# Raw first weights loaded by an account of bytes, and their narrowed halves split by ScalarE and GpSimd, in a talking-heads attention with two feed-forward layers

## The chip, the cores and the metric

The kernel runs on one core of a Trainium2 chip. The metric is device time in microseconds (us). Engines are named as in the profile: PE is the matrix engine (PEld its weight loads), DVE is VectorE, ACT is ScalarE, POOL is GpSimd, SP issues most of the DMAs; SPq and POOLq are the queues of DMA issues on SP and GpSimd.

## What is computed

```python
scores = einsum('bhij,hg->bgij', scale * q @ k.T, w_pre)      # batch 4, 12 heads, 448 positions, 64 wide
attn = exp(scores - max); attn = attn / (sum(attn) + 1e-9)
x = einsum('bhij,hg->bgij', attn, w_post) @ v                 # as 1792 tokens x 768
h = x @ w_in                                                  # w_in 768 x 1024
solu = h * softmax(h)
x = ((solu - mean) / sqrt(var + 1e-6) * g_ln) @ w_out         # w_out 1024 x 768
out = relu(x @ w2_in)**2 @ w2_out                             # 768 x 2048 and 2048 x 768
```

The four weight matrices of the two layers reach the kernel as 64-bit numbers. The program narrows them to 32 bits by shifts and masks. The layers' products are taken with each operand as a high part and a low part (`hi`, `lo`).

## The kernel before

**Work units.** The attention is cut into 16 chunks of 120 or 88 query rows. A chunk's scores of all heads are laid out in `ssrc`; DMAs then gather them, 9 or 10 query rows x 12 heads at a time, into 180 blocks (`sdst`, `shuffle`, L214). Two blocks make a pair, and a loop (L563) runs over slots; slot `s` is the turn that finishes pair `s`, for s = 0 to 89.

**One slot** issues, in this order: loads of keys, queries and values that are due; the gathers of pair s+5 (SP queue, 2 x 210 KB); a store of a finished chunk (`x_out`); at most one raw load of the first layer's weights (`load_w1`, POOL queue, 256 KB); the first mix over heads for pair s+2 (`pre`, PE, L237); the copies of pair s-1's result out of PSUM (`post_out`, DVE, L321 and L326); products of queries and keys for a later chunk (`qk`, PE L203, ACT L210); maximum (DVE L248) and exponential (ACT L255) of pair s+2; in about every third slot half a chunk's product with the values (`av`, PE L341); the weights of the second mix for pair s+1 (`weigh`); the steps of the narrowing; and the second mix of pair s (`post`, PE L302, 64 matmuls). Since every pair has just 64 matmuls of L302, the first of them dates the slot in the trace. The engines take their instructions in order, and each may run ahead of the others as far as the data allow.

**Narrowing the first layer's weights.** There are 48 pieces of 128x256. A piece is loaded (`load_w1`, at most six ahead of the narrowing), squared by ACT two slots later (`start_w1`, L76), shifted and masked by three DVE steps that `filler()` hands out (L79, L83, L87; five calls in a slot with `av`, two in the first six slots), finished by two POOL operations (`flush`, L96, L97), scaled by ACT where it belongs to `w_out` (L410), and stored to memory (`store_w1`, SP queue, 128 KB). Raw, square and result live in rings of 7, 4 and 7 buffers.

**Splitting the narrowed weights.** `prep_first` (L421) reads `w_in` back in 24 pieces of 256 columns and two token tiles of x in three pieces each. For a piece it issues the load (SP), and five steps later a cast to `hi` (ACT and DVE in turn, L450) and a subtraction to `lo` (POOL, L451). Six steps run after the last narrowed piece is stored, the rest four to a slot from slot 80 on, when the memory of keys and queries is free. The first product of the layer (`h1`, L463) starts in slot 88.

**`weigh`** (L262) takes the reciprocal of the row sums and scales `w_post` by it: three POOL operations (L266, L267, L273), but for the last seven pairs two DVE operations and two of ACT:

```python
        if s < tail:                                     # tail = NP - 7
            nc.gpsimd.tensor_scalar(...)                 # L266
            nc.gpsimd.tensor_tensor(..., op=ALU.pow)     # L267
        else:
            nc.vector.tensor_scalar(...)                 # L269
            nc.vector.reciprocal(sm, sm)                 # L270
```

After slot 90 the two layers follow (L640 on), which the change does not touch.

Of the kernel before, what the change touches and what calls it, by code (L numbers as in the profile page):

```python
# [18 lines left out]
def kernel(  # L19
# [129 lines left out]
    tail = NP - 7  # L149
# [112 lines left out]
    def weigh(s):  # L262

        sm = sms.pop(s)
        if s < tail:
# [6 lines left out]
        if s < tail:
            nc.gpsimd.tensor_tensor(  # L273
                out=w.rearrange("p b g i -> p b (g i)"),
                in0=wpost_bd.rearrange("p g i -> p (g i)").unsqueeze(1).to_broadcast([128, 2, H * RH]),
                in1=sm.unsqueeze(2).to_broadcast([128, 2, H * RH]),
                op=ALU.mult,
            )
# [115 lines left out]
    def narrow_w1(i):  # L394
# [24 lines left out]
    QW = 256  # L419

    def prep_first():  # L421

# [4 lines left out]
        for i in range(len(todo) + ahead):
            if i < len(todo):
                cc, u = todo[i]
                r = wi1_p.tile([128, QW], F32, tag="wraw", name="wraw", bufs=6)  # L430
                if cc is not None:
                    if u == 0:
                        w1i.append((wi1b_p if cc else wi1_p).tile([128, 2, F1], F32R, name=f"w1i{cc}"))
                    t = w1i[cc]
                    src = w1iD[cc * 128:(cc + 1) * 128, u * QW:(u + 1) * QW]
                    dst = [t[:, a, u * QW:(u + 1) * QW] for a in range(2)]
                    nc.sync.dma_start(out=r, in_=src)
                    rv = r
                else:
                    x, u = divmod(u, 3)  # L440
                    if u == 0:
                        xs[x] = (wi1b_p if x else wi1_p).tile([128, 2, CC, 128], F32R, name=f"xs{x}")
                    src = xD[u * 256:(u + 1) * 256, x * 128:(x + 1) * 128].rearrange("(c p) t -> p c t", p=128)
                    dst = [xs[x][:, a, 2 * u:2 * u + 2] for a in range(2)]
                    rv = r.rearrange("p (c t) -> p c t", c=2)
                    nc.sync.dma_start(out=rv, in_=src)
# [116 lines left out]
    for s in range(lo_s, NP + 2):  # L563
# [471 lines left out]
```

## Time and profile before

| | |
|---|---|
| three runs | 1133.25, 1137.06, 1140.11 us, median 1137.06 us |
| profiled execution | 1139.47 us, of which the profile's span is 1137.6 us |
| slots 0 to 87 (attention) | from 26.74 to 405.82 us of the span |
| after them | 731.78 us |
| mean granted clock of PE | 0.983 of full speed |

The profiled execution is one execution of the same program on the chip. Times inside it count from the start of the span. A busy share is that of one engine; the DMA share is the mean of the core's 16 DMA engines. A wait is put down to what came last before it ended, and "issue" means that the profile shows nothing that the engine waited for.

### The profile page before, as it was taken

The page shows a single profiled execution, that of the slowest core. Times are in us where ns is not written, and L with a number is a line of the kernel's source. Part 1 is how long each engine was busy: PE and PEld are TensorE (multiplying, and loading weights), DVE is VectorE, ACT ScalarE, POOL GpSimd, SP SyncE. Part 2 cuts the span into 40 slices and gives each one's busy share as a digit, 9 for nine tenths or more (in the row PEclk, how much of TensorE's full clock was granted, in tenths as well). Part 3 has the DMA queues.
Part 4 walks back from the last instruction along what each step waited for, and adds up shares of the span by engine and source line. Part 5 has one row for each costly group of instructions (what it writes and reads, how often), then busy time and mean ns, then how long its engine had stood idle before and what let it go on. Part 6 is the DMA issues. An engine that isn't in the chain of part 4 may idle for free.

```text
span 1137.6 us, 30858 instructions
## 1 busy us (share of the span) xinstructions
PE 1071.6 (94%) x12920; PEld 926.1 (81%) x12920; DVE 687.8 (60%) x1230; ACT 469.8 (41%) x1041; POOL 411.7 (36%) x637
## 2 busy tenths in 40 slices
PE   8788887988999699999999999999999999999998
PEld 2455655555666477889899999999999999999998
DVE  2756776786565647535343587366667676766734
ACT  4555655765766534312122366322232322323211
POOL 2686898887453626311010364011111111111100
PEclk9989999998999999999999999999999999999999
DMA  5886788787675533111110564011112121121113
GB/s 149 226 233 211 228 238 239 213 259 208 179 214 149 172 104 111 57 56 35 50 42 15 177 191 132 29 56 56 56 43 66 47 56 56 56 56 51 33 70 125
DMA packets 98507, 135.00 MB, mean 119 GB/s; under 512 B 21984, under 2 KB 84704, under 8 KB 98368
## 3 DMA queue, kind: packets, MB, share of 16 engines
q1 hardware_dynamic: 90432, 110.16, 32.5%
q0 software_dynamic: 6336, 22.22, 7.1%
q8 instruction: 102, 1.67, 0.6%
q10 hardware_dynamic: 1600, 0.64, 0.2%
q14 instruction: 37, 0.30, 0.1%
HBM read 71.65 MB, written 22.81 MB: 83 GB/s over the span
## 4 chain that ended last, share of the span: by engine, by line
PE 69%; DVE 2%; DMA 1%; issue 1%; ACT 1%; POOL 0%; SPq 0%; DVEq 0%; POOLq 0%; ACTq 0%
PE ps_h L899 21%; PE ps_y L938 21%; PE ps_o L745 10%; PE ps_h L463 10%; PE ps_ring L341 2%; PE ps_ring L302 2%; PE ps_pre L237 1%; PE ps_ring L203 1%; PE ps_tr L731 1%; DMA wraw<-w1iD 1%; DMA xD<-xt 0%; DVE nm L248 0%; ACT ssrc L210 0%; DVE at L321 0%; ACT e L255 0%
## 5 line engine op out<-in xcount | busy, mean ns | idle before, releaser
L899 PE MATMUL ps_h<-x,ti 128*128 128x384 f32 (+1 forms) x1440 | 241.5, 325 | 0.0
L938 PE MATMUL ps_y<-to,g 128*128 128x384 f32 x1332 | 240.0, 337 | 0.0
L899 PEld LDWEIGHTS ps_h<-x,ti 128*128 128x128 f32 x1440 | 236.5, 188 | 0.0
L938 PEld LDWEIGHTS ps_y<-to,g 128*128 128x128 f32 x1332 | 232.2, 188 | 1.7 <-DVE y L949 1.7
L302 PEld LDWEIGHTS ps_ring<-w,e 60*64 60x64 f32 (+1 forms) x5760 | 102.7, 138 | 77.0 <-issue 37.4
L321 DVE COPY at<-ps_ring 128x420 f32<-128x420 f32 x156 | 87.7, 610 | 99.4 <-PE ps_ring L302 99.3
L302 PE MATMUL ps_ring<-w,e 60*64 60x60 f32 (+2 forms) x5760 | 110.7, 222 | 37.7 <-issue 21.8
L907 ACT ACTIVATE r<-ps_h 128x384 f32<-128x384 f32 (+1 forms) x80 | 37.6, 470 | 215.4 <-PE ps_h L899 215.4
L210 ACT COPY ssrc<-ps_ring 128x896 f32<-128x896 f32 x93 | 83.3, 907 | 103.5 <-PE ps_ring L203 79.2
L463 PE MATMUL ps_h<-w1i,xs 128*128 128x512 f32 x504 | 120.5, 396 | 0.0
L745 PE MATMUL ps_o<-zt,w1o 128*128 128x384 f32 (+1 forms) x720 | 119.9, 325 | 0.0
L255 ACT ACTIVATE e<-ps_pre,nm 128x448 f32<-128x448 f32 x180 | 113.2, 639 | 14.9 <-DVE nm L248 14.9
L745 PEld LDWEIGHTS ps_o<-zt,w1o 128*128 128x128 f32 x720 | 116.8, 189 | 0.0
L908 DVE SCALAR_TENSOR_TENSOR r<-ps_h,r 128x384 f32<-128x384 f32 (+1 forms) x80 | 42.4, 530 | 122.9 <-ACT r L907 122.9
L463 PEld LDWEIGHTS ps_h<-w1i,xs 128*128 128x128 f32 x504 | 94.2, 188 | 21.6
L949 DVE TENSOR_TENSOR y<-ps_y,y 128x768 f32<-128x768 f32 x97 | 92.4, 952 | 31.8 <-PE ps_y L938 31.8
L248 DVE TENSOR_REDUCE nm<-ps_pre 128x1 f32<-128x448 f32 x180 | 103.2, 611 | 13.5 <-PE ps_pre L237 13.5
L203 PE MATMUL ps_ring<-k,q 64*64 64x448 f32 x768 | 103.6, 567 | 7.4 <-ACT ssrc L210 3.5
L855 POOL TENSOR_TENSOR ti<-wt,ti 128x384 fp32r<-128x384 f32 x32 | 34.7, 1083 | 205.6 <-ACT ti L854 205.5
L237 PE MATMUL ps_pre<-sdst,wpre_bd 64*64 64x448 f32 x720 | 102.3, 581 | 6.9 <-DMA sdst<-ssrc 4.4
L341 PEld LDWEIGHTS ps_ring<-at,v 128*64 128x64 f32 x1536 | 78.8, 142 | 33.0 <-PE ps_pre L237 12.0
L341 PE MATMUL ps_ring<-at,v 128*64 128x120 f32 (+1 forms) x1536 | 86.5, 270 | 8.4 <-issue 4.5
(89 smaller groups left out, 1192.1 us busy)
## 6 DMA issues: line engine op xcount, KB each, us to landing
sdst<-ssrc SPq DMA_DIRECT2D x172, 210.0 KB
wr<-in_moe_w_in_dram SPq DMA_DIRECT2D x32, 384.0 KB
wr<-in_moe_w_out_dram SPq DMA_DIRECT2D x32, 384.0 KB
w1raw<-in_moe_w_in_dram POOLq DMA_DIRECT2D x24, 256.0 KB, 6.6
w1raw<-in_moe_w_out_dram POOLq DMA_DIRECT2D x24, 256.0 KB, 5.4
out_dram<-y SPq DMA_DIRECT2D x13, 384.0 KB
v<-in_v_dram POOLq DMA_DIRECT2D x12, 384.0 KB, 6.6
xraw<-xD SPq DMA_DIRECT2D x12, 384.0 KB
```

Of the source, the lines that this page charges most:

```text
L203: nc.tensor.matmul(out=ps[64 * u:64 * u + 64, e, 0:S], lhsT=qq[c][64 * e:64 * e + 64, p * n + u * half:p * n + u * half + 64], rhs=k[64 * ...
L237: nc.tensor.matmul(out=ps[b][64 * u:64 * u + 64, 0:S], lhsT=wpre_bd[64 * r:64 * r + m], rhs=ds[b][64 * r:64 * r + m], start=True, stop=True,)
L248: nc.vector.tensor_reduce(out=nm, in_=pres[s][b][:, 0:S], op=ALU.max, axis=AX.X, negate=True)
L255: nc.scalar.activation(out=e, in_=pres[s][b][:, 0:S], func=AF.Exp, bias=nms.pop((s, b)), scale=1.0, accum_out=sms[s][:, b:b + 1])
L302: nc.tensor.matmul(out=ps[64 * c:64 * c + 64, u, i0:i0 + ng * RH], lhsT=e[64 * u:64 * u + m, o:o + 64], rhs=w[64 * u:64 * u + m, b, g0:g0 ...
L321: nc.vector.tensor_copy(dst[:, 1:3] if u else dst[:, 0:4:3], pv)
L341: nc.tensor.matmul(out=ps[64 * e:64 * e + 64, 0, q * 120:q * 120 + n], lhsT=t[:, g] if j < NJ else t[:, e, p], rhs=at[c][:, j * H + (g if ...
L463: nc.tensor.matmul(out=ps[:, u], lhsT=t[:, a, cc], rhs=w1i[cc][:, w, u * 512:(u + 1) * 512], start=(cc == 0 and a == 0 and w == 0), stop=( ...
L745: nc.tensor.matmul(out=ps[:, 0:width], lhsT=w1o[k][:, w, cc * 128:(cc + 1) * 128], rhs=zT[:, a, k, 0:width], start=(k == 0 and i == 0), st ...
L899: nc.tensor.matmul(out=ps[:, 0:n], lhsT=ti[:, w, cc, f * 128:(f + 1) * 128], rhs=x2[q][:, a, cc], start=(cc == 0 and i == 0), stop=(cc == ...
L938: nc.tensor.matmul(out=ps[:, u - us[0], 0:DM // 2], lhsT=g[:, a, f, o:o + 128], rhs=to[:, w, f, u * (DM // 2):(u + 1) * (DM // 2)], start= ...
L949: nc.vector.tensor_tensor(out=yo, in0=po, in1=yo, op=ALU.add)
```

## The change

Three things change, all in the attention part.

1. **When raw pieces are loaded.** An account runs from slot 5: each slot adds an equal share of bytes (that of all pieces, a load and a store of 384 KB in sum each, and of the other transfers of slots 5 to 63) and takes off what the slot moves of keys, values, queries and results. A piece is loaded when 384 KB have gathered, two in a slot at most, seven ahead of the narrowing at most. The square comes three slots after the load or later, with at most four pieces between square and the end of the POOL step. The DVE steps are handed out in slots with `av` alone, seven calls there; the generator now yields after the third step too, so seven calls are seven steps, which is also what five calls gave before.
2. **`weigh`** uses the three POOL operations for all pairs.
3. **`prep_first`** works in 12 pieces of 512 columns and two whole token tiles (128x768), two steps ahead with three buffers instead of five with six. `hi` is cast by ACT alone. One step runs in each of the slots 76 to 78 and 80 to 84, two in a slot from 85 on.

What the two loops issue, counted from the code (raw loads of 256 KB, stores of narrowed pieces of 128 KB, steps of `prep_first` that load):

| slots | loads before | loads after | stores before | stores after | split loads before | split loads after |
|---|---|---|---|---|---|---|
| 0 to 6 | 7 | 0 | 1 | 0 | 0 | 0 |
| 7 to 12 | 6 | 3 | 5 | 0 | 0 | 0 |
| 13 to 60 | 35 | 42 | 41 | 36 | 0 | 0 |
| 61 to 78 | 0 | 3 | 1 | 12 | 6 of 128 KB | 384 KB and 2 of 256 KB |
| 80 to 87 | 0 | 0 | 0 | 0 | 24 of 128 KB | 384 KB and 10 of 256 KB |

```diff
@@ narrow, narrow_w1: a yield after the last VectorE step
-        if eng is nc.vector:
-            yield True
+        yield True
+        if eng is nc.vector:
...
-        yield from narrow(w1raw.pop(i), sq, t, nc.gpsimd)
-        w1f[i] = sq, t
+        for step, _ in enumerate(narrow(w1raw.pop(i), sq, t, nc.gpsimd)):
+            if step == 3:
+                w1f[i] = sq, t
+            yield True
@@ weigh
-    tail = NP - 7
...
         sm = sms.pop(s)
-        if s < tail:
-            nc.gpsimd.tensor_scalar(out=sm, in0=sm, scalar1=1e-9, scalar2=None, op0=ALU.add)
-            nc.gpsimd.tensor_tensor(out=sm, in0=sm, in1=eps_sb[:, 2:3].to_broadcast([128, 2]), op=ALU.pow)
-        else:
-            nc.vector.tensor_scalar(out=sm, in0=sm, scalar1=1e-9, scalar2=None, op0=ALU.add)
-            nc.vector.reciprocal(sm, sm)
+        nc.gpsimd.tensor_scalar(out=sm, in0=sm, scalar1=1e-9, scalar2=None, op0=ALU.add)
+        nc.gpsimd.tensor_tensor(out=sm, in0=sm, in1=eps_sb[:, 2:3].to_broadcast([128, 2]), op=ALU.pow)
...
-        for b in (0, 1):
-            if s >= tail:
-                nc.scalar.activation(out=w[:, b], in_=wpost_bd, func=AF.Copy, scale=sm[:, b:b + 1])
@@ prep_first
-    QW = 256
+    QW = 512
...
-        todo = [(None, u) for u in range(3)] + [(cc, u) for cc in range(CC) for u in range(F1 // QW)]
-        todo[8:8] = [(None, u) for u in range(3, 6)]
-        ahead = 5
+        todo = [(None, 0), (0, 0), (0, 1), (1, 0), (1, 1), (None, 1)]
+        todo += [(cc, u) for cc in range(2, CC) for u in range(F1 // QW)]
+        ahead = 2
...
-                r = wi1_p.tile([128, QW], F32, tag="wraw", name="wraw", bufs=6)
+                r = wi1_p.tile([128, CC * 128], F32, tag="wraw", name="wraw", bufs=3)
...
-                (nc.scalar.copy if i % 2 else nc.vector.tensor_copy)(hi, rv)
+                nc.scalar.copy(hi, rv)
                 nc.gpsimd.tensor_tensor(out=lo, in0=rv, in1=hi.bitcast(F32), op=ALU.subtract)
             yield True
@@ the attention's loop
+    kb = {load_k: 448, load_v: 384, load_q: 360, x_out: 360}
+    moved = {s: sum(kb.get(f, 0) for f, a in js) for s, js in jobs.items()}
+    first_w1, last_w1 = 5, 64
+    share = (384 * len(w1pieces) + sum(moved.get(s, 0) for s in range(first_w1, last_w1))) / (last_w1 - first_w1)
+    room = owed = begun = 0
...
-        if s >= 0 and len(w1at) < len(w1pieces) and len(w1at) - kept < 6:
-            load_w1(len(w1at))
-            w1at.append(s)
+        if first_w1 <= s:
+            room += share - moved.get(s, 0)
+        while room >= 384 and owed < len(w1pieces):
+            room -= 384
+            owed += 1
+        for _ in range(2):
+            if len(w1at) < owed and len(w1at) - kept < 7:
+                load_w1(len(w1at))
+                w1at.append(s)
...
-        for i, z in enumerate(w1at):
-            if z == s - 2:
-                start_w1(i)
+        while begun < len(w1at) and w1at[begun] <= s - 3 and len(fill) + len(w1f) < 4:
+            start_w1(begun)
+            begun += 1
...
-        for _ in range(5 if any(f is av for f, a in js) else 2 if s < 6 else 0):
+        for _ in range(7 if any(f is av for f, a in js) else 0):
             filler()
...
-        kept = len(w1at) - len(fill) - sum(z > s - 2 for z in w1at)
+        kept = begun - len(fill)
...
         if last_raw is not None and last_raw < s <= min(last_qk, last_raw + 3):
             next(prep)
-            next(prep)
         if s > last_qk:
-            for _ in range(4):
+            for _ in range(1 if s < NP - DS else 2):
                 next(prep, None)
```

In program order the change shows as follows. First GpSimd in slots 3 to 5, where `w1raw` is a raw piece and `sm`, `w` belong to `weigh`. Before:

```order
L181 DMA v<-in_v_dram 128x768
L391 DMA w1raw<-in_moe_w_in_dram 128x256
L266 TENSOR_SCALAR sm<-sm 128x2
L267 TENSOR_TENSOR sm<-sm,eps_sb 128x2
L273 TENSOR_TENSOR w<-wpost_bd,sm 128x120
L181 DMA v<-in_v_dram 128x768
L391 DMA w1raw<-in_moe_w_in_dram 128x256
```

and now:

```order
L180 DMA v<-in_v_dram 128x768
L264 TENSOR_SCALAR sm<-sm 128x2
L265 TENSOR_TENSOR sm<-sm,eps_sb 128x2
L267 TENSOR_TENSOR w<-wpost_bd,sm 128x120
L180 DMA v<-in_v_dram 128x768
```

The raw loads that stood behind each load of values are gone from here.

Second GpSimd from slot 81 on before, and from slot 84 on now; `w1i` and `xs` are the `lo` halves of weights and of a token tile. Before:

```order
L266 TENSOR_SCALAR sm<-sm 128x2
L267 TENSOR_TENSOR sm<-sm,eps_sb 128x2
L273 TENSOR_TENSOR w<-wpost_bd,sm 128x120
L451 TENSOR_TENSOR w1i_5541<-wraw,w1i_5541 128x256 x2
L451 TENSOR_TENSOR w1i_6809<-wraw,w1i_6809 128x256
L451 TENSOR_TENSOR xs_6814<-wraw,xs_6814 128x256 x3
```

and now:

```order
L441 TENSOR_TENSOR xs_6947<-wraw,xs_6947 128x768
L264 TENSOR_SCALAR sm<-sm 128x2
L265 TENSOR_TENSOR sm<-sm,eps_sb 128x2
L267 TENSOR_TENSOR w<-wpost_bd,sm 128x120
L441 TENSOR_TENSOR w1i_7008<-wraw,w1i_7008 128x512 x2
L264 TENSOR_SCALAR sm<-sm 128x2
```

The subtractions, which before ran there one behind the other, now stand between the operations of `weigh` of every slot.

Third DVE from slot 81 on. Before:

```order
L321 COPY at<-ps_ring 128x2x42x5 x2
L248 TENSOR_REDUCE nm<-ps_pre 128x1 x2
L269 TENSOR_SCALAR sm<-sm 128x2
L270 RECIPROCAL sm<-sm 128x2
L450 CAST xs_6814<-wraw 128x256
L450 CAST w1i_6809<-wraw 128x256
L321 COPY at<-ps_ring 128x2x42x5 x2
```

and now:

```order
L312 COPY at<-ps_ring 128x2x42x5 x2
L247 TENSOR_REDUCE nm<-ps_pre 128x1 x2
L317 COPY at<-ps_ring 128x42x5 x4
L247 TENSOR_REDUCE nm<-ps_pre 128x1 x2
L312 COPY at<-ps_ring 128x2x42x5 x2
```

Between the copies out of PSUM and the maxima nothing else stands on DVE any more.

## Rows read from the trace of the kernel before

**Rows 1.** Windows of slots 0-6, 7-12, 13-60, 61-78, 79-87 and the rest; first line names columns.

```profile
core 0: us, PE busy (x) PEld busy (x) DVE busy (x) ACT busy (x) POOL busy (x), PEclk, DMA share, GB/s
26.74:64.61 37.87, 28.68 (x610) 18.13 (x609) 22.06 (x47) 18.27 (x44) 26.13 (x49) 0.87 0.81 228
64.61:95.38 30.77, 24.49 (x584) 16.37 (x584) 18.08 (x38) 18.20 (x43) 22.08 (x40) 0.94 0.85 243
95.38:304.14 208.76, 181.66 (x4690) 123.14 (x4688) 146.25 (x316) 139.44 (x330) 165.74 (x292) 0.96 0.77 221
304.14:368.37 64.23, 61.86 (x1730) 42.20 (x1729) 38.30 (x77) 42.08 (x97) 28.05 (x63) 1.00 0.64 184
368.37:405.82 37.45, 25.79 (x788) 18.79 (x784) 26.07 (x67) 22.39 (x66) 23.16 (x35) 0.95 0.58 167
405.82:1137.60 731.78, 727.25 (x4392) 700.73 (x4392) 429.58 (x673) 219.07 (x448) 140.03 (x134) 1.00 0.23 69
```

**Rows 2.** Timeline of PE: the posts that open slots 0, 7, 13, 61, 79, 80, 88.

```profile
26.74 1.13 PE L302 MATMUL ps_ring<-w,e 60*64 60x60 f32 x64
...
64.61 1.30 PE L302 MATMUL ps_ring<-w,e 60*64 60x60 f32 x64 [0.17 <-ACT ssrc L210]
...
95.38 1.13 PE L302 MATMUL ps_ring<-w,e 60*64 60x60 f32 x64
...
301.53 2.68 PE L341 MATMUL ps_ring<-at,v 128*64 128x120 f32 x48
304.14 1.13 PE L302 MATMUL ps_ring<-w,e 60*64 60x60 f32 x64
305.10 0.96 PE L237 MATMUL ps_pre<-sdst,wpre_bd 64*64 64x448 f32 x8
...
368.37 1.13 PE L302 MATMUL ps_ring<-w,e 60*64 60x60 f32 x64
...
370.08 1.11 PE L302 MATMUL ps_ring<-w,e 60*64 60x60 f32 x64
...
405.82 1.13 PE L302 MATMUL ps_ring<-w,e 60*64 60x60 f32 x64 [1.46 <-ACT w L281]
```

**Rows 3.** Waits of PE from 26.74 to 304.14: total us, times, longest.

```profile
PE ps_ring L302 <- issue: 21.2, 12, 4.6
...
PE ps_pre L237 <- ACT w1sq L76: 1.7, 1, 1.7
PE ps_ring L203 <- ACT w1sq L76: 1.5, 1, 1.5
```

**Rows 4.** Groups of instructions, 20 to 410: count | busy us, mean ns | idle before.

```profile
L267 POOL TENSOR_TENSOR sm<-sm,eps_sb 128x2 f32<-128x2 f32 x83 | 62.0, 747 | 6.9
...
L273 POOL TENSOR_TENSOR w<-wpost_bd,sm 128x120 f32<-128x120 f32 x83 | 33.1, 399 | 6.5
...
L76 ACT ACTIVATE w1sq<-w1raw 128x256 f32<-128x256 f32 x48 | 21.4, 445 | 14.4 <-POOL w1t L97 10.7 <-DMA w1raw<-in_moe_w_in_dram 2.8 <-POOL sm L266 0.7
L266 POOL TENSOR_SCALAR sm<-sm 128x2 f32<-128x2 f32 x83 | 19.8, 238 | 88.6 <-ACT e L255 85.3
...
L451 POOL TENSOR_TENSOR w1i<-wraw,w1i 128x256 fp32r<-128x256 f32 x24 | 17.3, 734 | 9.7 <-DVE w1i L450 4.6 <-ACT w1i L450 4.3 <-DMA wraw<-w1iD 0.9
...
L450 DVE CAST w1i<-wraw 128x256 fp32r<-128x256 f32 x13 | 6.1, 477 | 10.9 <-DMA wraw<-w1iD 7.4 <-issue 3.5
...
L281 ACT ACTIVATE w<-wpost_bd,sm 128x60 f32<-128x60 f32 x14 | 4.0, 340 | 0.7 <-DVE sm L270 0.7
...
L269 DVE TENSOR_SCALAR sm<-sm 128x2 f32<-128x2 f32 x7 | 1.4, 196 | 0.0
L270 DVE RECIPROCAL sm<-sm 128x2 f32<-128x2 f32 x7 | 1.2, 166 | 0.2
```

**Rows 5.** Waits of PE from 368.37 to 405.82: total us, times, longest.

```profile
PE ps_ring L302 <- ACT w L281: 6.8, 3, 3.3
PE ps_ring L302 <- DVE at L321: 1.7, 1, 1.7
```

More of the change, by code (lines that the diff above doesn't have):

```diff
@@ L264, in weigh @@
         sm = sms.pop(s)
-        if s < tail:
-            nc.gpsimd.tensor_scalar(out=sm, in0=sm, scalar1=1e-9, scalar2=None, op0=ALU.add)
-            nc.gpsimd.tensor_tensor(out=sm, in0=sm, in1=eps_sb[:, 2:3].to_broadcast([128, 2]), op=ALU.pow)
-        else:
-            nc.vector.tensor_scalar(out=sm, in0=sm, scalar1=1e-9, scalar2=None, op0=ALU.add)
-            nc.vector.reciprocal(sm, sm)
-        w = late_p.tile([128, 2, H, RH], F32, tag="w", name="w", bufs=3)
[L272 to L278, printed above, removed]
-        for b in (0, 1):
-            if s >= tail:
-                nc.scalar.activation(out=w[:, b], in_=wpost_bd, func=AF.Copy, scale=sm[:, b:b + 1])
+        nc.gpsimd.tensor_scalar(out=sm, in0=sm, scalar1=1e-9, scalar2=None, op0=ALU.add)
+        nc.gpsimd.tensor_tensor(out=sm, in0=sm, in1=eps_sb[:, 2:3].to_broadcast([128, 2]), op=ALU.pow)
+        w = late_p.tile([128, 2, H, RH], F32, tag="w", name="w", bufs=3)
+        nc.gpsimd.tensor_tensor(
+            out=w.rearrange("p b g i -> p b (g i)"),
+            in0=wpost_bd.rearrange("p g i -> p (g i)").unsqueeze(1).to_broadcast([128, 2, H * RH]),
+            in1=sm.unsqueeze(2).to_broadcast([128, 2, H * RH]),
+            op=ALU.mult,
+        )
         ws[s] = w
@@ L433, in prep_first @@
                         w1i.append((wi1b_p if cc else wi1_p).tile([128, 2, F1], F32R, name=f"w1i{cc}"))
[L434 to L438, printed above, removed]
-                else:
[L440 to L446, printed above, removed]
+                    rv = r[:, 0:QW]
+                    dst = [w1i[cc][:, a, u * QW:(u + 1) * QW] for a in range(2)]
+                    nc.sync.dma_start(out=rv, in_=w1iD[cc * 128:(cc + 1) * 128, u * QW:(u + 1) * QW])
+                else:
+                    xs[u] = (wi1b_p if u else wi1_p).tile([128, 2, CC, 128], F32R, name=f"xs{u}")
+                    rv = r.rearrange("p (c t) -> p c t", c=CC)
+                    dst = [xs[u][:, a] for a in range(2)]
+                    nc.sync.dma_start(
+                        out=rv, in_=xD[:, u * 128:(u + 1) * 128].rearrange("(c p) t -> p c t", p=128)
+                    )
                 loaded.append((rv, dst))
```

## The prediction

> **What bounds the kernel now.** I read the windows first, cut at slot borders. [...] The reader should compare two of them. In slots 61 to 78, where no raw weights are loaded, 18 slots take 64.23 us, 3.57 us a slot, with PE busy for 61.86 us at full clock: PE bounds, and the DMA engines move 184 GB/s, 0.66 MB a slot. In slots 13 to 60 the same work takes 208.76 us for 48 slots, 4.35 us a slot, at 221 GB/s, 0.96 MB a slot; PE is idle for 27 us there and the clock is at 0.96. Slots 7 to 12 take 5.13 us each at 243 GB/s and a DMA share of 0.85, slots 0 to 6 take 5.41 us each at 228 GB/s. So the more bytes a slot moves, the longer it is. The waits of PE say how: of what it lost from slot 0 to slot 60, 21.2 us in 12 stalls stand before matmuls of posts with nothing missing that the profile shows ("issue"), up to 4.6 us at once; 3.2 us are behind ACT's square of a raw piece [rows 3]. The end of the attention, slots 79 to 87, is something else: DMA share 0.58, PE busy for 25.79 of 37.45 us [rows 1]. There PE waits 6.8 us for the weights from ACT [rows 5], and DVE, which comes before ACT in that chain, stood 10.9 us before its casts of `w1i` [rows 4]. What follows slot 88 is PE at 727 of 732 us [rows 1] and is not touched.
>
> **The change part by part.** The sum is made against the profiled execution, 1139.47 us.
>
> *Loads moved out of slots 0 to 12.* The code issues 7 loads and 1 store less in slots 0 to 6 (7 x 0.262 + 0.131 = 1.97 MB), and 3 loads and 5 stores less in slots 7 to 12 (1.44 MB). Slots 0 to 6 hold no `av`, so PE has less to do than later; it is busy for 28.68 of 37.87 us although the clock there is the lowest of all stages, 0.87 [rows 1], and I take it that bytes set the pace. At that stage's 228 GB/s the 1.97 MB are 8.6 us. From slot 7 on PE has its full work, and there I take the slope between the two long stages: (4.35 - 3.57) us for (0.96 - 0.66) MB, 2.6 us a MB. That gives 3.7 us for 1.44 MB; at the plain rate of 243 GB/s it would be 5.9 us. Sum: **-12.3 us**, between 0 (if something other than bytes sets these slots) and -14.5.
>
> *The same bytes in later slots.* Slots 13 to 60 get 7 loads more and 5 stores less, +1.18 MB: at 2.6 us a MB **+3.0 us** (at 221 GB/s 5.3). Slots 61 to 78 get 3 loads, 11 stores and 0.13 MB of split loads more, +2.36 MB, 0.79 MB a slot instead of 0.66. By the slope that is 6.1 us. PE is the bound there and could hide all of it (0), or the stage could fall to the pace of slots 13 to 60, 18 x 0.78 = 14 us. Of the added bytes 1.44 MB are stores, for which no engine of the attention waits, so I take two thirds of the slope: **+4 us**.
>
> [...]
>
> *The narrowing's own steps.* 48 squares, 144 DVE steps, 96 POOL operations and 24 scalings stay as many as they were; seven calls of `filler` hand out as many steps in an `av` slot as five did, because the generator yields once more. Nothing for these. What falls is the waiting of ACT: its 48 squares stood idle 10.7 us for a buffer that POOL had not given back and 2.8 us for a raw piece [rows 4]. ACT is in order, and the copies of scores and the exponentials queue behind. Starting three slots after the load, with at most four pieces under way, takes both away. PE's rows show 3.2 us of it [rows 3]; the rest was hidden or stands under "issue". **-3.2 us**, between 0 and -13.5. The new limit of seven loads makes POOL wait now and then for the DVE step that frees a raw buffer; behind it stands `weigh` of the next pair, needed a slot later, 2.5 us or more, so nothing.
>
> *The end, slots 80 to 87.* DVE loses its casts and seven reciprocals; ACT gets all casts and loses 14 scalings of 0.34 us; POOL gets `weigh` in every slot, 0.238 + 0.747 + 0.399 = 1.38 us [rows 4]. A subtraction of 512 columns I price at twice that of 256, 1.47 us, one of 768 at three times, 2.2 us [rows 4]. PE needs 1.13 + 0.96 = 2.1 us a slot and 2.68 more with `av`, 4.8 [rows 2]. POOL needs 1.38 + 1.47 = 2.9 us in a slot with one step, 3.6 with the token tile, 4.3 with two. Taking the larger of the two for the eight intervals from post 80 to post 88 (`av` in slots 81, 84 and 87): 4.8 + 2.9 + 2.9 + 4.8 + 3.6 + 4.3 + 4.8 + 4.3 = 32.4 us. Before it was 405.82 - 370.08 = 35.7 [rows 2]. **-3.3 us**. At best all PE waits of [rows 5] go, -8.5; at worst +5, if the loads land late: SP's next load waits for POOL's subtraction one step before, and the gathers of the coming pairs are queued behind that load on SP; on ACT the exponentials and the copies of `av` are queued behind a cast that waits for its load.
>
> [...]
>
> *Sum:* -12.3 + 3.0 + 4 - 3.2 - 3.3 = -11.8, so 1127.7 us for an execution like the profiled one. That one lies 2.4 us above the median of the runs, 1137.06; off the median I forecast **1125 us**, 1.0% less. About 0.5%, 5.7 us, is what a measurement of this kernel can tell from no change.
>
> **The rivals.** *All the waits go* (1104 us). With the load of bytes evened out, the low clock stretches and the squares' waits vanish, bytes are hidden in slots 61 to 78, and the end runs at PE's pace: -14.5 + 3.0 + 0 - 13.5 - 8.5 = -33.5, less 2.4. For it speaks that the clock is at 1.00 wherever bytes are few [rows 1]; against it that in slots 13 to 60, most of the time, bytes rise a little.
>
> *Bytes bind nowhere* (1130 us). The "issue" stalls come by themselves, and only the waits and the end count: -3.2 - 3.3 = -6.5. [...] For it: the share is never 1 over a stage. Against it: the stage without raw loads has nearly none of the stalls, PE idle 2.4 us in 64 [rows 1].
>
> *The clean stage is lost* (1147 us, slower). The raw loads now reach to slot 65 and the stores to slot 75. If slots 61 to 78 fall to 4.35 us each, +14 us, and the loop of three buffers (load, ACT, POOL, next load) holds up the end by +5, while the start gains its 12.3, slots 13 to 60 lose 3.0 and no wait of ACT goes: +9.7. With the other terms as here it ends over 0.5% slower once these slots take more than 4.1 us each on the mean. Against it: share 0.64 there, so the added bytes make some 0.77 of it, and PE has the lead.
>
> *The account does not even anything out* (1137 us): two loads in one slot beside a load of values are 1.3 MB, as many as in the worst slots of before, and the stalls only move.
>
> **How the numbers follow.** Forecast 0.53, all waits go 0.10, bytes bind nowhere 0.20, clean stage lost 0.10, nothing evened out 0.07. The border of 0.5% is at 1131.4 us below and 1142.7 above. The forecast's own spread, 1115 to 1133, gives faster 0.9 of the time; bytes bind nowhere gives it 0.6 of the time. Faster: 0.48 + 0.10 + 0.12 = 0.70; same 0.05 + 0.08 + 0.07 = 0.20; slower 0.10. The range runs from 1108 to 1140 us: it leaves out most of the two outer rivals, 0.2 in all.
>
> **What would show it.** Right: in the changed profile slots 0 to 12 take about 56 us instead of 68.6; slots 13 to 60 some 212, slots 61 to 78 some 68; "issue" stalls fall in the first and appear in the last; ACT's squares wait for nothing; from slot 80 to 88 32 us, with POOL and not DVE as what PE waits for. Wrong: slots 0 to 12 as long as before (bytes did not set them), slots 61 to 78 over 75 us, or the end over 36 us with ACT or SP standing before loads of `wraw`.

## The result, and the profile after

The changed kernel took 1127.72 us (median) beside 1135.88 us for the kernel before in the same comparison: a ratio of **0.9892, interval 0.9851 to 0.9934**, 12.3 us less (7.5 to 16.9). This ratio leaves out the longest of the changed kernel's four runs, 1137.16 us, which counts as slow because it lies over 1.5% above the fastest, although its granted clock of 0.985 is like that of the others (0.984 to 0.992); the two medians, with all runs in them, give 0.9928, 8.2 us less. Forecast were 1125 us, 1.0% less. Its profiled execution took 1130.63 us, 8.8 us less than that of the kernel before. First the windows of the changed kernel, cut at its own posts like [rows 1]: slots 0 to 6, 7 to 12, 13 to 60, 61 to 78, 79 to 87, and the rest.

```profile
26.01:59.41 33.40, 26.62 (x617) 17.49 (x609) 16.21 (x29) 17.32 (x42) 16.49 (x36) 0.85 0.71 192
59.41:84.24 24.83, 22.30 (x586) 14.57 (x584) 15.30 (x30) 15.85 (x35) 15.15 (x31) 1.00 0.83 221
84.24:298.54 214.30, 183.89 (x4690) 124.83 (x4688) 146.74 (x318) 135.83 (x321) 162.56 (x292) 0.95 0.76 226
298.54:365.95 67.41, 62.57 (x1730) 42.12 (x1729) 46.86 (x102) 48.43 (x115) 47.08 (x83) 1.00 0.71 209
365.95:395.41 29.46, 24.35 (x789) 18.40 (x785) 19.37 (x40) 20.40 (x51) 23.69 (x37) 1.00 0.64 182
395.41:1128.80 733.39, 728.82 (x4392) 702.01 (x4392) 428.86 (x670) 219.81 (x448) 146.37 (x140) 1.00 0.23 70
```

Against [rows 1] slots 0 to 12 are 10.4 us shorter (68.64 to 58.23), slots 13 to 60 are 5.5 longer, slots 61 to 78 are 3.2 longer, and slots 79 to 87 are 8.0 shorter. The rest differs by 1.6. Next the waits of PE (total us, times, longest): first slots 0 to 60, then 61 to 78, then 79 to 87; they answer to [rows 3, 5].

```profile
PE ps_ring L293 <- issue: 22.9, 14, 4.3
PE ps_ring L293 <- POOL w L267: 2.0, 3, 1.1
...
PE ps_ring L293 <- issue: 3.5, 4, 1.1
...
PE ps_ring L293 <- POOL w L267: 4.8, 3, 2.9
```

The "issue" stalls before matmuls of posts (now L293) did not fall: 21.2 us before and 22.9 now, of which 5.7 and 5.3 in slots 0 to 12. In the end PE no longer waits for weights from ACT, but for those from POOL. Of the groups, the squares (L76, slots 0 to 87) and, from post 80 to post 88, the casts and subtractions of `prep_first` (columns as in [rows 4]):

```profile
L76 ACT ACTIVATE w1sq<-w1raw 128x256 f32<-128x256 f32 x48 | 19.7, 442 | 0.3 <-POOL w1t L97 0.3
...
L441 POOL TENSOR_TENSOR w1i<-wraw,w1i 128x512 fp32r<-128x512 f32 x9 | 11.4, 1274 | 2.5 <-ACT w1i L440 2.5
L440 ACT CAST w1i<-wraw 128x512 fp32r<-128x512 f32 x10 | 6.2, 620 | 3.4 <-DMA wraw<-w1iD 3.4
```

The squares wait for nothing, as forecast. A subtraction of 512 columns takes 1.27 us (priced at 1.47). The last row is the one to remember: casts stand 3.4 us before loads of `wraw`, the buffers of `prep_first`. In the kernel before it was 7.4 us on DVE (of the 10.9 us that its casts stood idle, [rows 4]) and 6.6 us on ACT (shown below).

### The profile page after: what moved, and what is told of

It reads as the page before. It is cut to its first block, busy times and chain, and to the rows that moved or that the text cites. A ratio compares the mean times of both kernels' runs of the same rounds, so it can differ in the third digit from the quotient of the medians.

```text
span 1128.8 us, 30803 instructions
## 1 busy us (share of the span) xinstructions
PE 1068.8 (95%) x12920; PEld 925.7 (82%) x12920; DVE 680.3 (60%) x1201; ACT 468.3 (41%) x1026; POOL 417.8 (37%) x642
## 4 chain that ended last, share of the span: by engine, by line
PE 86%; issue 4%; POOL 3%; DMA 3%; ACT 2%; DVE 1%; SPq 1%; POOLq 0%; ACTq 0%; DVEq 0%
PE ps_h L899 21%; PE ps_y L938 21%; PE ps_o L745 10%; PE ps_h L453 10%; PE ps_ring L293 7%; PE ps_ring L332 6%; PE ps_pre L236 5%; PE ps_ring L202 5%; DMA sdst<-ssrc 2%; PE ps_tr L731 1%; ACT ssrc L209 1%; POOL sm L265 1%; ACT e L254 1%; POOL w1sq L96 0%; POOL w1t L97 0%
## 5 line engine op out<-in xcount | busy, mean ns | idle before, releaser
L293 PEld LDWEIGHTS ps_ring<-w,e 60*64 60x64 f32 (+1 forms) x5760 | 105.0, 140 | 75.8 <-issue 46.2
L293 PE MATMUL ps_ring<-w,e 60*64 60x60 f32 (+2 forms) x5760 | 113.3, 225 | 34.6 <-issue 26.6
L247 DVE TENSOR_REDUCE nm<-ps_pre 128x1 f32<-128x448 f32 x180 | 103.3, 612 | 13.1 <-PE ps_pre L236 12.8
L332 PEld LDWEIGHTS ps_ring<-at,v 128*64 128x64 f32 x1536 | 75.1, 138 | 29.8 <-PE ps_pre L236 12.7
L332 PE MATMUL ps_ring<-at,v 128*64 128x120 f32 (+1 forms) x1536 | 82.2, 263 | 7.5 <-issue 5.4
```

The lines of the kernel that those rows point to most:

```text
L247: nc.vector.tensor_reduce(out=nm, in_=pres[s][b][:, 0:S], op=ALU.max, axis=AX.X, negate=True)
L293: nc.tensor.matmul(out=ps[64 * c:64 * c + 64, u, i0:i0 + ng * RH], lhsT=e[64 * u:64 * u + m, o:o + 64], rhs=w[64 * u:64 * u + m, b, g0:g0 ...
L332: nc.tensor.matmul(out=ps[64 * e:64 * e + 64, 0, q * 120:q * 120 + n], lhsT=t[:, g] if j < NJ else t[:, e, p], rhs=at[c][:, j * H + (g if ...
```

## The experiments

Ratios are to the kernel before, timed beside each. All use the unchanged code of the kernel before or of the changed one but for the edit shown.

**The two halves apart.** `e_pace` has the account of bytes alone, `e_end` has `weigh` and `prep_first` alone.

```diff
# e_pace: before, with these parts of the change
+        if first_w1 <= s:
+            room += share - moved.get(s, 0)
...
+        while begun < len(w1at) and w1at[begun] <= s - 3 and len(fill) + len(w1f) < 4:
...
+        for _ in range(7 if any(f is av for f, a in js) else 0):
# e_end: before, with these
# weigh: three POOL operations for every pair, as in the change
+    QW = 512
+        ahead = 2
+                nc.scalar.copy(hi, rv)
...
+            for _ in range(1 if s < NP - DS else 2):
```

> The kernel before with only the account of bytes, the later squares and the seven filler steps; weigh and prep_first as they were. Theory A (the end alone pays: the stage times of the changed kernel summed to -7.2 us for slots 0 to 78 against -8.0 for slots 79 to 87, but one profile each can be off by some us): the pacing only moves time from the first 13 slots to the later ones, 1134 to 1137 us against 1136. Theory B (the pacing pays what the prediction's terms say, -12.3 + 3.0 + 4 - 3.2 = -8.5): 1127 us. Both expect slots 80 to 88 to stay at 35 to 36 us with PE waiting there for the weights from ACT, and ACT's squares to wait less than 1 us for buffers instead of 13.5.

> The kernel before with only weigh on POOL and the new prep_first with its calls; raw loads as they were. Theory A: 1127 to 1129 us, with slots 80 to 88 at 27 us instead of 35.7 and everything before slot 79 as in the kernel before (slots 0 to 12 at 68 us, 13 to 60 at 209, 61 to 78 at 64). Theory B (the end is worth its term, -3.3): 1132 to 1133 us, with slots 80 to 88 at 32 us; the 27 us of the changed kernel would then need its evened loads.

`e_pace`: **0.9965 [0.9937, 0.9994]**, 4.0 us less (0.7 to 7.2). `e_end`: **0.9931 [0.9910, 0.9953]**, 7.8 us less (5.3 to 10.2). The product, 0.9896, agrees with the ratio of the whole change, 0.9892, though its interval of 9 us cannot show that the halves add up to the us. Each expectation held in part. The end is worth about what theory A said, with 27 us from post 80 to 88 and loads as they were. But it is not alone: the account pays too, though half of the 8.5 us of theory B. Windows of `e_pace` (slots 0 to 6, 7 to 12, 13 to 60, 61 to 78, then post 80 to 88), and of `e_end` the last alone:

```profile
26.75:58.04 31.29, 24.66 (x612) 15.77 (x609) 15.72 (x29) 16.95 (x41) 16.27 (x35) 0.89 0.74 201
58.04:82.87 24.83, 22.47 (x584) 14.59 (x584) 15.30 (x30) 16.85 (x39) 15.38 (x32) 1.00 0.80 215
82.87:293.45 210.58, 183.22 (x4690) 123.06 (x4689) 146.00 (x318) 135.75 (x321) 163.34 (x292) 0.95 0.78 229
293.45:360.08 66.63, 62.45 (x1730) 42.18 (x1729) 46.99 (x102) 47.94 (x115) 46.03 (x85) 1.00 0.71 207
361.79:397.53 35.74, 24.27 (x717) 17.58 (x709) 23.58 (x64) 21.14 (x64) 23.03 (x35) 0.95 0.59 169
```

```profile
371.11:398.50 27.39, 23.39 (x717) 18.16 (x709) 17.92 (x37) 19.08 (x48) 22.36 (x33) 0.94 0.65 195
```

The end is untouched by the account (35.74 us, as in [rows 2]) and takes 27.39 without it. A stage of one execution wanders by some us, so the account's effect on the stages is better read from all the profiles: seven kernels load as the kernel before (itself, `e_end` and five below) and three as the changed one (itself, `e_pace`, `c_mix`). Means, with the extremes:

| | loads as before | loads by the account | difference |
|---|---|---|---|
| slots 0 to 12 | 67.5 (63.5 to 69.1) | 58.8 (56.1 to 62.0) | -8.7 |
| slots 13 to 60 | 208.5 (204.2 to 211.4) | 211.1 (208.4 to 214.3) | +2.6 |
| slots 61 to 78 | 65.6 (63.9 to 67.6) | 68.6 (66.6 to 71.9) | +3.0 |

They sum to -3.1 us, which agrees with the 4.0 that were timed. Only in slots 0 to 12 do the two groups stand apart; in the other stages their extremes overlap, so +2.6 and +3.0 are uncertain. `e_end`, for one, takes 67.61 us in slots 61 to 78 with the loads as before.

**The squares' waits alone.**

```diff
# e_sq: before, with
-        if s >= 0 and len(w1at) < len(w1pieces) and len(w1at) - kept < 6:
+        if s >= 0 and len(w1at) < len(w1pieces) and len(w1at) - kept < 7:
...
-        for i, z in enumerate(w1at):
-            if z == s - 2:
-                start_w1(i)
+        while begun < len(w1at) and w1at[begun] <= s - 3 and len(fill) + len(w1f) < 4:
+            start_w1(begun)
+            begun += 1
```

> The kernel before with only the later squares (three slots after the load, at most four pieces under way, seven loads ahead); no account of bytes, weigh and prep_first as they were. The prediction's term for ACT's waits: the squares' 13.5 us of idle time go and the time falls by 3.2 us, 1133 us. The rival, which the changed kernel's slots 13 to 60 suggest (+5.5 us although the squares wait for nothing): the squares' waits go and PE loses the same time as issue stalls, 1136 us.

**0.9995 [0.9969, 1.0021]**: no gain is seen, as the rival had it, but the interval, 3.5 us less to 2.4 more, just takes in the 3.2 us of the forecast. The squares' idle time is gone, and "issue" before posts is 24.5 us in slots 0 to 60, against 21.2 in the kernel before:

```profile
L76 ACT ACTIVATE w1sq<-w1raw 128x256 f32<-128x256 f32 x48 | 19.2, 443 | 0.5 <-POOL w1t L97 0.5
```

```profile
PE ps_ring L302 <- issue: 24.5, 16, 4.3
```

That is more than the 18.2 to 21.4 us of the seven kernels with the loads and squares as before, so part of PE's wait may have moved there. One profile does not show it: `c_mix`, where the squares wait for nothing either, has 15.9. Nor is PE's wait for squares a steady one: of those seven profiles, it is 3.2 us in the kernel before, 1.8 in `e_acthi`, 1.5 in `e_alt` and nothing in `e_end`, `e_weigh`, `e_prep` and `e_burst`.

**What the raw loads cost.**

```diff
# e_noraw: the changed kernel, with
     def load_w1(i):
         src, dst, k, o = w1pieces[i]
+        if i >= 7:
+            w1raw[i] = first7[i % 7]
+            return
...
+        first7.append(t)
```

> The changed kernel with 41 of the 48 raw loads left out (10.7 MB): pieces 8 to 48 are narrowed from the first seven raw buffers over again, so all steps of ACT, DVE and POOL and all stores remain, and the weights of the first layer are wrong. Theory B (bytes set the pace of slots 13 to 60): by the slope of 2.6 us a MB 28 us less, 1100 us, slots 13 to 60 at 186 us, the issue stalls of PE nearly gone and the clock at 0.99 or more. Theory C (bytes bind nowhere; the stalls and the low clock come by themselves): 1125 to 1128 us, slots 13 to 60 still over 208 us with 20 us or more of issue stalls.

**0.978 [0.9749, 0.9812]**. That is 1.13% or 12.8 us below the changed kernel (by the two intervals, some 6 us either way), for 10.7 MB: 1.2 us a MB, half of the slope that the prediction used. Leaving out the loads pays, against theory C, but half as much as theory B had it, and most of the stalls stay. The windows are slots 13 to 60 and 61 to 78, the waits those of slots 0 to 60:

```profile
85.61:275.84 190.23, 173.51 (x4690) 117.34 (x4688) 146.54 (x318) 135.75 (x321) 141.98 (x254) 1.00 0.69 200
275.84:343.25 67.41, 61.82 (x1730) 41.95 (x1729) 47.40 (x102) 48.47 (x115) 45.04 (x81) 1.00 0.68 198
```

```profile
PE ps_ring L293 <- issue: 14.6, 12, 2.3
```

Slots 13 to 60 fall from 214.30 to 190.23 us at a clock of 1.00 instead of 0.95, close to the 186 expected. These are two single executions: the 24 us are about twice what was timed, and 10.4 of them are PE's own busy time at the higher clock (183.89 to 173.51). And 14.6 of 22.9 us of "issue" stalls are still there. Nor are bytes all that went. POOL issues these loads, at 0.6 us each in the trace of the changed kernel, and its busy time in slots 13 to 60 falls from 162.56 to 141.98 us, so not all of its steps remain, as the expectation has it. PE waits only 2.0 us for POOL in slots 0 to 60 of the changed kernel, so this is probably a small part, but bytes and issues were not tried apart. Slots 61 to 78, which lost only 3 of the left-out loads, take 67.41 us in both kernels, so raw loads do not explain the 3 us by which they are longer than in [rows 1]; what does was not tried.

**What held the end.** Six kernels take the end apart.

```diff
# e_weigh: before, with weigh in three POOL operations for every pair
# e_acthi: e_weigh, and
-                (nc.scalar.copy if i % 2 else nc.vector.tensor_copy)(hi, rv)
+                nc.scalar.copy(hi, rv)
# e_prep: before, with the new prep_first and its calls; weigh as before
# e_alt: e_prep, and
-                nc.scalar.copy(hi, rv)
+                (nc.scalar.copy if i % 2 else nc.vector.tensor_copy)(hi, rv)
# e_burst: e_prep, and
-            for _ in range(1 if s < NP - DS else 2):
+            for _ in range(2):
# c_mix: the changed kernel, with weigh as before, the casts of e_alt, and
-            for _ in range(1 if s < NP - DS else 2):
+            for _ in range(2 if s in (NP - 10, NP - 7, NP - 4) else 1):
```

> The kernel before with only weigh on POOL for the last seven pairs; casts still on ACT and DVE in turn, 256 columns a step. Theory A1 (PE waited for the order on DVE, whose reciprocals stood behind its casts): the 6.8 us of PE behind ACT's weights go, slots 80 to 88 take 28 to 30 us, 1129 to 1130 us. Theory A2 (POOL is in order too, so its weigh now stands behind subtractions that wait for DVE's casts): the wait only changes its name, slots 80 to 88 stay at 34 to 36 us, 1135 to 1137 us, and PE waits for POOL instead. [...]

> The kernel before with weigh on POOL and the casts on ACT alone, but still 256 columns a step, five steps ahead, four steps to a slot. Theory A (what counts is that DVE is out of the chain): slots 80 to 88 at 27 to 29 us, 1127 to 1130 us. Theory E (the spreading of the steps counts: four subtractions of 0.73 us and 1.38 us of weigh are 4.3 us of POOL in each slot while steps last): slots 80 to 88 at 31 to 34 us with POOL as what PE waits for, 1132 to 1136 us.

> The kernel before with only the new prep_first (512 columns, casts on ACT alone) and its calls; weigh stays on DVE and ACT for the last seven pairs, raw loads as they were. Theory A (DVE's casts in front of its reciprocals were the cause; weigh could have stayed): slots 80 to 88 at 27 to 29 us instead of 35.7, 1127 to 1130 us. Theory D (both parts are needed, since ACT now has all casts, 0.6 us each, in front of its 14 scalings): PE still waits 4 us or more for the weights from ACT, slots 80 to 88 at 31 to 34 us, 1132 to 1135 us.

> The new prep_first alone (512 columns, one or two steps a slot), but with its casts on ACT and DVE in turn as before; weigh stays on DVE and ACT, raw loads as they were. Theory A (the end was held by DVE's casts in front of its reciprocals, as the prediction read it): PE waits again for the weights from ACT, slots 80 to 88 at 32 us or more, 1132 us or more. Theory G (the end is held by how the steps are cut and spread; which engine casts is nothing): slots 80 to 88 at 27 to 28 us, 1128 to 1130 us.

> The new prep_first alone (512 columns, casts on ACT, weigh on DVE and ACT), but two steps in every slot from 80 on, which is the 1024 columns a slot of the kernel before, instead of one in slots 80 to 84. Theory G1 (the spreading counts: two subtractions of 1.28 us, or 1.82, and two casts a slot are more than a slot without av, 1.74 us, can hide): slots 80 to 88 at 31 to 36 us, 1132 to 1136 us. Theory G2 (the longer pieces count, with half as many steps and a subtraction of 1.28 us in place of two of 0.73): 27 to 29 us, 1128 to 1130 us.

> The changed kernel's account of bytes and its 512-column steps, but weigh for the last seven pairs on DVE and ACT and the casts on ACT and DVE in turn, both as in the kernel before, and two steps at the end of slots 80, 83 and 86, which runs beside an av, with one in every other slot. Theory G (only the cutting and spreading of the steps counts, and the account of bytes): at least as fast as the changed kernel, slots 80 to 88 at 24 to 26 us instead of 27.25, 1124 to 1128 us, 0.986 to 0.990 of the kernel before. Rival H (with evened loads the moves of weigh and casts are needed after all): slots 80 to 88 at 28 us or more, 1129 us or more.

The table sets the time from post 80 to post 88 beside what casts on ACT and DVE stood there before loads of `wraw` (the idle time put down to those loads; the rows follow), and PE's busy time and granted clock in that window. "Lead" is how many slots before its cast a load is issued: `ahead` steps by steps a slot.

| | ratio | 80 to 88, us | casts before loads, us | PE busy, us, at clock | lead |
|---|---|---|---|---|---|
| before | 1 | 35.74 | 14.0 | 24.08 at 0.95 | 1.25 |
| `e_weigh` | 1.0028 [1.0009, 1.0048] | 36.63 | 20.3 | 25.39 at 0.91 | 1.25 |
| `e_acthi` | 1.0030 [1.0010, 1.0049] | 36.73 | 12.8 | 27.90 at 0.81 | 1.25 |
| `e_burst` | 0.9984 [0.9959, 1.0008] | 33.99 | 9.4 | 25.89 at 0.85 | 1 |
| `c_mix` | 0.9944 [0.9917, 0.9970] | 30.27 | 7.2 | 25.02 at 0.89 | 1 to 2 |
| `e_end` | 0.9931 [0.9910, 0.9953] | 27.39 | 2.4 | 23.39 at 0.94 | 2, then 1 |
| after | 0.9892 [0.9851, 0.9934] | 27.25 | 3.4 | 22.41 at 1.00 | 2, then 1 |
| `e_prep` | 0.9928 [0.9902, 0.9955] | 27.03 | 2.1 | 22.01 at 1.00 | 2, then 1 |
| `e_alt` | 0.9945 [0.9928, 0.9962] | 25.95 | 0.6 | 22.37 at 1.00 | 2, then 1 |

Groups of casts in that window: of the kernel before those on ACT (6.6 us beside the 7.4 on DVE, [rows 4]), then of `e_weigh`, `e_acthi`, `e_burst` and `e_alt`:

```profile
L450 ACT CAST w1i<-wraw 128x256 fp32r<-128x256 f32 x11 | 4.4, 405 | 5.9 <-DMA wraw<-w1iD 5.9
L450 ACT CAST xs<-wraw 128x256 fp32r<-128x256 f32 x3 | 1.2, 400 | 0.7 <-DMA wraw<-xD 0.7
```

```profile
L441 DVE CAST w1i<-wraw 128x256 fp32r<-128x256 f32 x13 | 5.4, 422 | 12.2 <-DMA wraw<-w1iD 10.7 <-DMA xD<-xt 1.4
L441 ACT CAST w1i<-wraw 128x256 fp32r<-128x256 f32 x11 | 4.4, 409 | 6.8 <-DMA wraw<-w1iD 6.8
L441 ACT CAST xs<-wraw 128x256 fp32r<-128x256 f32 x3 | 1.2, 403 | 2.8 <-DMA wraw<-xD 2.8
```

```profile
L441 ACT CAST w1i<-wraw 128x256 fp32r<-128x256 f32 x24 | 9.3, 409 | 10.0 <-DMA wraw<-w1iD 10.0
L441 ACT CAST xs<-wraw 128x256 fp32r<-128x256 f32 x5 | 1.9, 405 | 2.8 <-DMA wraw<-xD 2.8
```

```profile
L447 ACT CAST w1i<-wraw 128x512 fp32r<-128x512 f32 x12 | 7.2, 618 | 7.3 <-DMA wraw<-w1iD 7.2
L447 ACT CAST xs<-wraw 128x768 fp32r<-128x768 f32 x1 | 0.8, 833 | 2.2 <-DMA wraw<-xD 2.2
```

```profile
L447 ACT CAST w1i<-wraw 128x512 fp32r<-128x512 f32 x4 | 2.4, 610 | 0.6 <-DMA wraw<-w1iD 0.6
L447 DVE CAST w1i<-wraw 128x512 fp32r<-128x512 f32 x4 | 2.3, 580 | 0.0
```

The mechanisms of theories A2, E, A, G and G1 hold, in the order of the first five expectations, with two misses in the numbers and one in the reason. `e_weigh` and `e_acthi` came out slower than theories A2 and E had them, and slower than the kernel before (1139.57 and 1140.97 us). In both PE waits for weights from POOL, 8.1 and 8.8 us. `e_prep` met the time of theory A, but the reason that A gave, DVE's casts, falls with `e_alt`.

Three things follow. Moving `weigh` to POOL brings nothing: alone it costs 0.3%, and with the new steps it makes no difference (27.39 with it, 27.03 without). Which engine casts makes no difference that is clear of noise: `e_alt` gives half of the casts back to DVE and still takes 6.3 us less than the kernel before (4.3 to 8.2). How the steps are spread counts: with `e_burst`, which differs from `e_prep` in the calls alone, most of the gain is gone.

The time goes with the lead. With one slot or a little more the load lands after its cast has come to the head of an engine, and behind that cast stand exponentials, copies and the weights that PE waits for, since the engines take instructions in order. In `e_burst` ACT stood 2.09 us before a cast, came to the weights behind it at 379.22, and PE, 1.60 us idle for them, went on at 379.61:

```profile
376.45 0.62 ACT L447 CAST w1i<-wraw 128x512 fp32r<-128x512 f32 x1 [2.09 <-DMA wraw<-w1iD]
...
379.22 0.57 ACT L281 ACTIVATE w<-wpost_bd,sm 128x60 f32<-128x60 f32 x2
...
379.61 1.13 PE L302 MATMUL ps_ring<-w,e 60*64 60x60 f32 x64 [1.60 <-ACT w L281]
```

That the lead does it is argued from such rows and from the table. No run changes the lead alone, as `e_burst` also puts two casts and two subtractions into a slot. Against that as the cause speaks that over the window ACT is busy for 23.19 and POOL for 19.44 of 33.99 us, while casts stand 9.4 us before loads. The casts' idle time is a rough measure: `e_pace` and `e_sq`, whose end is that of the kernel before, have 19.7 and 19.1 us of it where that has 14.0, in 35.74 and 35.26 us. And the clock has a share: it is at 1.00 in `e_prep`, `e_alt` and the changed kernel, and between 0.81 and 0.95 in the others, where PE is itself busy for longer. Of the 7.0 us between `e_burst` and `e_prep` 3.9 are PE's busy time.

`c_mix` missed its 24 to 26 us. The double step in slot 83 left a cast on DVE 4.56 us before its load, with the copies of posts (L321) behind it; PE waited 3.4 us for them:

```profile
387.18 0.43 DVE L449 CAST w1i<-wraw 128x512 fp32r<-128x512 f32 x1 [4.56 <-DMA wraw<-w1iD]
387.53 1.14 DVE L321 COPY at<-ps_ring 128x420 f32<-128x420 f32 x2
```

So PE's longest slots were not where a second step is free. The numbers are those of rival H (28 us or more, 1129 us or more), that with evened loads the moves of `weigh` and casts are needed after all. The kernel differs from the change in `weigh`, casts and calls at once. The late cast speaks for the calls, but with the account of bytes rival H was not tried by itself and stays open.

**Fewer bytes, after the attention.** If bytes cost 1.2 us a MB, and the layers leave DMA at a share of 0.23 and DVE at 429 of 733 us, then some pieces could be narrowed there.

```diff
# c_late: the changed kernel, with rows 640 to 1023 of w_out narrowed after the attention
+            for _ in narrow(lraw[i], sq, t):
+                pass
...
+            nc.scalar.activation(out=t, in_=t, func=AF.Copy, scale=g_sb[:, k:k + 1])
+            nc.scalar.copy(hi, t)
+            nc.gpsimd.tensor_tensor(out=lo, in0=t, in1=hi.bitcast(F32), op=ALU.subtract)
...
+        late_pieces(5 if m == 0 else 1 if m == 1 else 0)    # before norm1(m), one more after m >= 1
# c_late2: one piece in slot 88, two in 89, two in front of the last av, then
+            late_pieces(2 if m == 0 else 1)                 # for m < 2, and one after m = 2
```

> The changed kernel with the last 9 of the 48 pieces (rows 640 to 1023 of the second matrix, w_out) taken out of the attention: they are loaded raw, narrowed by ACT and DVE and split in the first four token tiles after it (slots 88 on, where DVE idles and the DMA share is 0.2 to 0.5), without the way through memory. Theory B (bytes of the attention cost what leaving out 10.7 MB of loads gave back, 12.9 us or 1.2 us a MB): 9 loads of 0.262 MB and 9 stores of 0.131 MB are 3.5 MB, 4.2 us less than the changed kernel, 1123 us. Theory F (DVE's 15 us of added steps delay the first tiles and give it back): 1127 us or more, with PE waiting for DVE or POOL between the attention's end and 460 us.

> The changed kernel with the same 9 pieces of w_out taken out of the attention as in the try before, but their squares and narrowing begun in slots 88 to 90, in front of the last products with the values, in a pool of their own; two pieces stand before the first normalisation instead of five, and none in the third tile. Theory B (the 3.5 MB less are worth what the attention lost in the try before, 4 to 8 us, and the first tiles no longer wait): 1120 to 1124 us, with the time from slot 88 to the end within 3 us of the changed kernel's 733.4. Theory F (any DVE work there costs its time, as POOL's subtractions slow DVE's steps from 0.3 to 1.9 us): 1128 us or more, with 740 us or more after slot 88.

**1.0056 [1.0029, 1.0083]** and **1.0025 [0.9999, 1.0052]**: theory F. Up to post 88 the profile of `c_late` has more than the 4.2 us that were hoped for, 360.8 us from post 0 instead of 369.4. Then it lost more. Of each the window from post 88 to the end, first `c_late`, then `c_late2`:

```profile
387.63:1143.80 756.17, 736.79 (x4392) 708.21 (x4392) 450.24 (x706) 228.57 (x472) 146.62 (x146) 0.98 0.22 70
```

```profile
393.72:1145.50 751.78, 737.16 (x4392) 708.69 (x4392) 449.29 (x706) 228.83 (x472) 147.05 (x146) 0.99 0.23 70
```

That is 22.8 and 18.4 us more than in the changed kernel. Of these 8.0 and 8.3 us are PE's own busy time (728.82 in the changed kernel), at clocks of 0.98 and 0.99; most of the rest are waits. The timeline of DVE in `c_late`, and one row of PE, show the longest:

```profile
397.61 0.42 DVE L87 SCALAR_TENSOR_TENSOR lt<-lraw,lt 128x256 uint32<-128x256 uint32 x1
408.16 0.43 DVE L92 SCALAR_TENSOR_TENSOR lt<-lsq,lt 128x256 f32<-128x256 f32 x1 [10.12 <-ACT lsq L76]
...
416.92 1.21 DVE L730 TENSOR_REDUCE nm<-ps_h 128x1 f32<-128x1024 f32 x1
...
425.77 1.90 DVE L79 TENSOR_SCALAR lt<-lraw 128x256 uint32<-128x256 uint32 x1
427.70 1.93 DVE L83 SCALAR_TENSOR_TENSOR lt<-lraw,lt 128x256 uint32<-128x256 uint32 x1
...
426.10 1.94 PE L763 MATMUL ps_tr<-id_sb,e 128*128 128x128 f32 x8 [10.10 <-DVE e L746]
```

DVE stood 10.12 us before a square that ACT does behind the last copies of `av`. The first normalisation began at 416.92, and PE then waited 10.10 us for its result (the transposes at L763). DVE's idle time was there, but in the chain of the first tile. `c_late2` begins earlier and still held PE up, 4.7 us at the last `av` and 6.3 us in the first tiles.

## Why the forecast was right

The total was right, in part by luck: it is a sum of two errors of opposite sign. The account paid half of its term, the end more than twice its own, and the end did so by another mechanism than the one forecast.

- *Slots 0 to 12, forecast -12.3.* The means give -8.7 us, and the changed profile 58.23 us where 56 was written. The sign and the place were right. For 3.41 MB this is 2.6 us a MB. In slots 0 to 6, priced at the plain rate of 228 GB/s, the means give -4.2 us of the forecast -8.6; in slots 7 to 12, priced at the slope, -4.5 where -3.7 was forecast. The stalls of PE that were to fall there did not (5.7 and 5.3 us).
- *Slots 13 to 60, forecast +3.0.* The means give +2.6, with overlapping extremes.
- *ACT's waits, forecast -3.2.* **No run shows this term.** The squares' idle time went away entirely and the time stayed (`e_sq`, 0.9995, with an interval that just reaches 3.2 us). The price came from one profile, and there PE's two waits for squares stand in slots 0 to 12 (1.5 us in slots 0 to 6, 1.7 in 7 to 12), a stretch whose whole gain the first term already counted.
- *Slots 61 to 78, forecast +4.* +3.0, with overlapping extremes. The "issue" stalls appeared there as forecast, 0.7 us before and 3.5 after.
- *The account as a whole, forecast -8.5.* Timed: -4.0 (-7.2 to -0.7).
- *The end, forecast -3.3.* **Mis-sized**: timed -7.8 (-10.2 to -5.3), from post 80 to 88 27.25 us instead of 32.4. The steps were added slot by slot, the larger of PE and POOL in each. But POOL runs on across slots, and its 22.4 us of work fit in 27.25; the subtraction was 1.27 us, not 1.47; and a slot without `av` takes PE 1.74 us, not 2.1, since `pre` and `post` overlap:

```profile
372.65 1.13 PE L293 MATMUL ps_ring<-w,e 60*64 60x60 f32 x64
373.61 0.96 PE L236 MATMUL ps_pre<-sdst,wpre_bd 64*64 64x448 f32 x8
374.39 1.13 PE L293 MATMUL ps_ring<-w,e 60*64 60x60 f32 x61
```

- *What PE waited for in the end.* Here the mechanism was wrong. The prediction read a chain from DVE's casts to ACT's weights, and gave the gain to DVE's relief; `e_alt` leaves half of the casts on DVE, between its reciprocals, and keeps most of the gain. The row said more: the 10.9 us of DVE's casts had "DMA wraw" behind 7.4 of them [rows 4]. The loads were late, and the better spread steps gave them time. That PE would wait for POOL instead of ACT came true. For moving `weigh` off VectorE the forecast entered no cost of its own. By [rows 4] the three operations take 1.38 us on POOL, where those for the last seven pairs took 0.36 on DVE and 0.68 on ACT; seven times the difference is an estimated 2.4 us. Alone the move is 3.2 us slower (1.0 to 5.5; `e_weigh`), which takes in that estimate; with the new steps it makes no difference (`e_end` beside `e_prep`).
- *The rivals.* "Bytes bind nowhere" falls with `e_noraw`, as far as bytes and their issues can be taken as one, but half of it is true: most "issue" stalls stay without the raw loads. "The clean stage is lost" needed over 4.1 us a slot in slots 61 to 78; it was 3.7. "All the waits go" needed the stalls to vanish; its support, a clock of 1.00 wherever bytes are few, misreads [rows 1], which have 0.95 at 167 GB/s in slots 79 to 87. "The account evens nothing out" is against `e_pace`, though not by much.

What stays open is why slots 13 to 60 keep their stalls; the last section shows what they go with.

## What to carry to other kernels

Count the lead of a load in time, not in steps: if it is read by an in-order engine, a cast that waits for it holds up everything behind (in `e_burst` ACT for 2.09 us, and PE for 1.60), and fewer, evenly spread steps can be worth more than a faster or freer engine (`e_prep` 0.9928, `e_acthi` 1.0030). A wait that one profile shows need not be a gain when it goes; take it away alone, and look for it in a second profile, before it is entered as one. Idle shares of an engine over a long stage say nothing of the few microseconds where a chain goes through it.

## What the runs showed of the hardware

**"Issue" stalls follow the instruction queue.** In `e_noraw`, PE stopped in the middle of a post's 64 matmuls, with nothing that the profile shows it to wait for:

```profile
139.06 0.92 PE L293 MATMUL ps_ring<-w,e 60*64 60x60 f32 x48
141.64 0.38 PE L293 MATMUL ps_ring<-w,e 60*64 60x60 f32 x13 [1.65 <-issue]
```

The DMA view of the window 139.0 to 140.3 has one packet on the queue of instructions, beside gathers (queue, kind: packets, MB, share):

```profile
q1 hardware_dynamic: 151, 0.25, 61.3%
q8 instruction: 1, 0.02, 4.7%
```

PE went on 1.3 us after the end of that window. This is no single case. On that queue one packet of 16 KB comes every 5.3 us or so in the attention (median), and in the traces of all 14 kernels every "issue" stall of PE of 0.5 us or more between 26 and 396 us, 228 of them, ended 1.1 to 1.9 us after the end of such a packet; by chance some 15% would fall into that band of 0.8 us in 5.3. So PE seems to stand there for instructions, and the stalls seem to be the cases in which the packet came late: in the kernel before, 13 such stalls for 65 packets. Why a packet is late is not shown: those before stalls took 0.9 to 1.6 us in the kernel before, like the others (median 1.1), and no run changed the instructions. That the packet causes the stall is argued from the order of events.

**Two steps of DVE were long beside POOL.** In `c_late` the same shift (L79, 128x256) took 0.28 us, but 1.90 us when it came at 425.77, while POOL subtracted two inputs. The step behind it (L83), 0.42 us elsewhere, took 1.93. POOL's timeline:

```profile
425.26 4.09 POOL L675 TENSOR_TENSOR w1o<-w1oraw,w1o 128x768 fp32r<-128x768 f32 x2
```

The first of POOL's two subtractions (2.04 us each) ended at 427.3, the first of the DVE steps at 427.67; the second ended at 429.35, the second DVE step at 429.63. The step behind them (L87), after POOL's end, took 0.42 us. How POOL would hold them no trace shows; that it does is argued from these times.
